# Attention with a warm-up on the identity, later gates, one transpose of the factors and another tie rule, and two blocks written out behind an expert's first

## The chip, the cores and the metric

One core of a Trainium2 chip runs one launch of the kernel. The metric is the time of one execution on the device in microseconds. Three executions of the kernel before took 898.0, 899.84 and 900.85 us (median 899.84).

## The reference, cut to what matters

Three steps follow one another, all in float32 on random inputs.

```python
# attention: q, k, v are (4, 8, 576, 64); M_prev, z_prev are a memory of each head
a = softmax(causal(q @ k.T / 8));  local = a @ v           # sum of exp + 1e-9 in the divisor
q_p = where(q > 0, q, exp(q) - 1) + 1
mem_out = (q_p @ M_prev) / (q_p @ z_prev + 1e-6)
x = g * mem_out + (1 - g) * local                          # g = sigmoid(beta), one for each head
# dense layer: 2304 tokens x 512, width 2048
h = x @ w_in;  x = (h * tanh(softplus(h))) @ w_out
# experts: 8 of width 1024, each token goes to its best one, or is left as it is
active = x @ w_skip > 0;  e = argmax(x @ w_gate);  gate = softmax(x @ w_gate)[e]
out = x;  out[active] += gate * relu(x @ w1[e]) @ w2[e]
```

On the inputs of the reference 225, 124, 333, 54, 528, 206, 18 and 5 tokens go to experts 0 to 7.

## The kernel before, in words

**Attention** works on 16 pairs of heads, p = 0 to 15. A pair has the steps that `attention` adds to a planner (`Work`, from L840): loads on SP's queue (`ld`, `lq`, `lv`, L939), the scaling of q on POOL (`sq`, L1014), the memory's q_p and its row sums (`f1` to `f4`), four score steps on TensorE (`S0` for query tiles 0 and 1, `S2`, `S3`, `S4`; L1046 to L1054), the row maximum on VectorE (`pk`, L1060 and L1063), the exponential with its row sum on ScalarE (`ex`, L1074), the factors of each row (`s0`, `s1`, `s2`: 1/sum times 1-g or g), the memory's part beside the exponentials (`place`, L1100), TensorE transposes of the exponentials by query tile (`t0` to `t4`, `b0`; L1106) with their evictions (L1006 on VectorE, L1008 on ScalarE), and the products with v and M (`AV0`, `AV1`, L1134), which leave the pair's output, turned, in the PSUM tile `px`. Two PSUM slots serve the scores (`ps`) and two the transposes (`pt`).

The output is still to be scaled by the factors, which stand along partitions and are wanted along the free dimension. So `r` transposes them on TensorE, three times (even heads, odd heads, the last half tiles; L1112, L1113), `re` evicts them in two pieces to `rt_`, `rw` stores these with two transfers to DRAM (L1122, L1123), and `rs` reads them back, spread over 64 partitions for each head, with two transfers (L1127). `xe` copies `px` to SBUF (VectorE or ScalarE), `X` multiplies by the spread factors `R` on POOL (L1146), `xo` stores. The last pair goes the same way.

Between these steps runs the conversion of the first weight matrix of the dense layer (`cv`, 16 pieces; L792, L803, L813 to L837) and, near the end, the loading and splitting of the first two token blocks (`xs`).

**The planner's order.** Every step has an engine, a duration, a due time (`key`; pairs are 11.2 apart) and the steps that it needs. `Work.run` repeatedly takes the step with the lowest rank, and the plan's order is each engine's program order:

```python
rank = (round((start + turn) * 8), t[0], t[1])
```

`start` is the time from which engine, needs and slot are free, `turn` a switch cost of TensorE, `t[0]` the due time: steps within the same eighth of a microsecond go by due time. The first loads of pair 0 are not in the plan, so that its steps count as ready at time 0. The gates (`g0`, `g1`, L984 to L996) are due at 4 and 5.

Ahead of the plan, VectorE clears 512 columns of an exponential's buffer (L1264) and TensorE multiplies it by itself twice (`keep_warm`, L1262); both results are never read.

**The dense layer** (`moe`) follows: for each block of 256 tokens `gemm1` (L197 to L199), the activation on ScalarE (L209 to L222), `gemm2` (L249 to L251). The first 16 steps convert the second weight matrix on the way (`convert`: L805, L813 to L824, L834 on ScalarE, L837 on POOL).

**The experts.** Two blocks of 128 tokens of the fullest expert run at the end of the dense layer. Then a loop over the 8 experts computes a first block, always, with the next expert's weights being split in between. Behind it stand `NSTAT - 1` further blocks inside nested conditionals on the expert's number of blocks `nb[e]`, read at run time, and behind them, in one more conditional, a run-time loop for the rest:

```python
for j in range(1, NSTAT):
    stack.enter_context(tc.If(nb[e] > j))
    if j + 1 < NSTAT:
        nxt["g"] = gather(idx(e, j + 1), j % 2)     # and turn it during the block
    block(e, xg, xT, idx(e, j), gate(e, j), fill)
stack.enter_context(tc.If(nb[e] > NSTAT))
with tc.For_i(NSTAT, nb[e], 1) as j:
```

So each written-out block but the last gathers and turns the rows of the next one, whether that runs or not. With the token counts above (the fullest expert's first 256 taken out) the experts have 2, 1, 3, 1, 3, 2, 1 and 1 blocks: six blocks behind an expert's first, two of them third blocks, no fourth.

## Time and profile before

| | |
|---|---|
| three executions | 898.0, 899.84, 900.85 us |
| the profiled execution | 903.65 us, of which the span is 901.9 us |
| TensorE | 844.4 us busy (94%), 5412 matmul instructions |
| TensorE's weight loads | 687.3 us (76%) |
| ScalarE | 622.4 us (69%) |
| VectorE | 577.8 us (64%) |
| POOL | 278.4 us (31%) |
[...]

Shares of busy time are means over three different stages: attention to about 235 us, the dense layer to about 665 us, the experts to the end. A row of the timeline gives start, duration, engine, line, operation, output and inputs, the number of instructions merged, and in brackets how long the engine sat idle before it and what ended that. PEld is TensorE's weight load, PEq and PEldq its sequencer, SPq the queue of DMA issues.

### The profile page before, as it was taken

How to read it: one execution, taken by the hardware profiler on the slowest of the kernel's cores; microseconds unless marked ns; L12 is line 12 of the kernel's file. 1: busy time of each engine (PE TensorE's matmuls, PEld its weight loads, DVE VectorE, ACT ScalarE, POOL GpSimd, SP SyncE). 2: the span in 40 equal slices, each digit the busy share in tenths (PEclk: the TensorE clock that was granted, in tenths of full speed). 3: DMA queues.
4: the chain of work that ended last, by engine and by line, in shares of the span. 5: the costliest groups of instructions: out<-in, count | busy, mean ns of one | idle time of the engine just before them, and what ended most of it. 6: DMA issues, size and time to landing. Idle time of an engine off the chain costs nothing.

```text
span 901.9 us, 15116 instructions
## 1 busy us (share of the span) xinstructions
PE 844.4 (94%) x5412; PEld 687.3 (76%) x5412; DVE 577.8 (64%) x1171; ACT 622.4 (69%) x1136; POOL 278.4 (31%) x358
## 2 busy tenths in 40 slices
PE   5899999999889999999999999999988989989995
PEld 3566656666779998989898989888866867768774
DVE  6988878766488843356575757575558666373661
ACT  4687768876588887787878788787845555363551
POOL 5876776854223230110111111011103212211200
PEclk8999999999999999999999999999989999999998
DMA  6666657642333231010101010122336958284610
GB/s 211 192 197 206 200 168 230 214 143 87 123 94 110 94 129 49 24 47 24 48 24 48 25 48 24 48 94 95 95 125 211 349 197 288 67 288 151 198 62 4
DMA packets 53704, 113.44 MB, mean 126 GB/s; under 512 B 12148, under 2 KB 17396, under 8 KB 53600
## 3 DMA queue, kind: packets, MB, share of 16 engines
q1 hardware_dynamic: 43968, 91.22, 31.3%
q0 software_dynamic: 4064, 10.42, 3.5%
q10 hardware_dynamic: 5568, 10.49, 3.2%
q8 instruction: 56, 0.92, 0.4%
q14 instruction: 48, 0.39, 0.1%
HBM read 94.47 MB, written 18.77 MB: 126 GB/s over the span
## 4 chain that ended last, share of the span: by engine, by line
PE 40%; DMA 21%; issue 15%; ACT 8%; POOL 7%; DVE 5%; SPq 1%; ACTq 0%; POOLq 0%; another core or an unknown queue 0%; DVEq 0%
DMA cvt<-yd,ids 8%; DMA out<-cvf,ids 6%; PE ph L197 6%; PE ph L199 6%; PE ph L198 6%; PE py L249 6%; PE py L251 6%; PE py L250 6%; DMA r<-rd 3%; DMA qn<-qn 2%; PE px L1134 2%; PE pt L1106 2%; POOL mn L1027 1%; ACT e L1074 1%; DVE nm L1063 1%
## 5 line engine op out<-in xcount | busy, mean ns | idle before, releaser
L197 PE MATMUL ph<-xh,u 128*128 128x256 f32 x576 | 163.8, 284 | 0.9 <-DVE xr L1006 0.9
L199 PE MATMUL ph<-xh,u 128*128 128x256 f32 x576 | 162.5, 282 | 0.0
L198 PE MATMUL ph<-xl,u 128*128 128x256 f32 x576 | 162.3, 282 | 0.0
L249 PE MATMUL py<-u,gh 128*128 128x512 f32 x288 | 115.8, 402 | 4.9 <-POOL u L837 4.9
L251 PE MATMUL py<-u,gl 128*128 128x512 f32 x288 | 115.7, 402 | 4.2 <-DVE gl L235 4.2
L250 PE MATMUL py<-u,gh 128*128 128x512 f32 x288 | 115.1, 400 | 0.0
L197 PEld LDWEIGHTS ph<-xh,u 128*128 128x128 f32 x576 | 109.8, 191 | 3.4 <-DVE xr L1006 1.1
L198 PEld LDWEIGHTS ph<-xl,u 128*128 128x128 f32 x576 | 109.8, 191 | 2.5
L199 PEld LDWEIGHTS ph<-xh,u 128*128 128x128 f32 x576 | 109.8, 191 | 0.0
L225 DVE SCALAR_TENSOR_TENSOR g<-t,g 128x512 f32<-128x512 f32 x72 | 49.9, 693 | 92.0 <-ACT t L221 89.8
L1074 ACT ACTIVATE e<-ps,nm 128x256 f32<-128x256 f32 (+4 forms) x144 | 78.0, 550 | 29.7 <-DVE nm L1063 21.9
L235 DVE TENSOR_TENSOR gl<-g,gh 128x512 fp32r<-128x512 f32 x72 | 51.1, 709 | 62.4 <-ACT gh L234 53.9
L1106 PE MATMUL pt<-ident,e 128*128 128x128 f32 x528 | 77.0, 285 | 8.3 <-ACT eta L1008 5.6
L351 POOL DMA_INDIRECT rt<-pay,sl x18 | 22.1, 1225 | 181.6 <-DVE pay L349 178.8
L209 ACT ACTIVATE g<-ph 128x512 f32<-128x512 f32 x72 | 42.7, 593 | 46.8 <-PE ph L199 45.8
L1106 PEld LDWEIGHTS pt<-ident,e 128*128 128x128 f32 x528 | 57.5, 143 | 18.6 <-ACT eta L1008 7.5
L251 PEld LDWEIGHTS py<-u,gl 128*128 128x128 f32 x288 | 54.9, 191 | 19.5 <-DVE gl L235 6.3
L249 PEld LDWEIGHTS py<-u,gh 128*128 128x128 f32 x288 | 55.2, 192 | 15.6 <-POOL u L837 5.0
L106 POOL TENSOR_TENSOR xl<-xr,xh 128x256 fp32r<-128x256 f32 x36 | 31.5, 880 | 112.0 <-ACT xh L105 111.8
L837 POOL TENSOR_TENSOR u<-cvf,u 128x512 fp32r<-128x512 f32 x32 | 46.6, 1458 | 58.6 <-ACT u L834 58.6
L250 PEld LDWEIGHTS py<-u,gh 128*128 128x128 f32 x288 | 54.9, 191 | 9.9
L1063 DVE TENSOR_REDUCE nm<-ps 128x2 f32<-128x256 f32 (+1 forms) x64 | 51.1, 816 | 7.0 <-PE ps L1054 6.1
(236 smaller groups left out, 1976.7 us busy)
## 6 DMA issues: line engine op xcount, KB each, us to landing
raw<-w SPq DMA_DIRECT2D x26, 512.0 KB
qk<-qk SPq DMA_DIRECT2D x16, 608.0 KB
raw<-w_in SPq DMA_DIRECT2D x16, 512.0 KB
raw<-w_out SPq DMA_DIRECT2D x16, 512.0 KB
xl<-w SPq DMA_DIRECT2D x16, 512.0 KB
xh<-w SPq DMA_DIRECT2D x15, 512.0 KB
qn<-qn SPq DMA_DIRECT2D x16, 384.0 KB
vx<-vx SPq DMA_DIRECT2D x16, 320.0 KB
```

What stands on the lines that cost most here:

```text
L197: T.matmul(ps[:, f2], win(HI, k, f), hi[:, k], start=(k == 0), stop=False)
L198: T.matmul(ps[:, f2], win(HI, k, f), lo[:, k], start=False, stop=False)
L199: T.matmul(ps[:, f2], win(LO, k, f), hi[:, k], start=False, stop=(k == KD - 1))
L225: V.scalar_tensor_tensor(out=g, in0=t, scalar=ROOT_HALF, in1=g, op0=ALU.add, op1=ALU.mult)
L235: V.tensor_tensor(out=gl, in0=g, in1=gh.bitcast(F32), op=ALU.subtract)
L249: T.matmul(ys[i][t], gh[:, f2, ts], wout(HI, f), start=(f == 0), stop=False)
L250: T.matmul(ys[i][t], gh[:, f2, ts], wout(LO, f), start=False, stop=False)
L251: T.matmul(ys[i][t], gl[:, f2, ts], wout(HI, f), start=False, stop=(f == KF - 1))
L837: self.nc.gpsimd.tensor_tensor(out=lo, in0=self.now.pop(i), in1=hi.bitcast(F32), op=ALU.subtract)
L1063: V.tensor_reduce(out=nm, in_=ps[:, :, o:o + w], axis=AX.X, op=ALU.max, negate=True)
L1074: A.activation(out=E[p % 2][:, k, 64:64 + w], in_=src, func=AF.Exp, bias=nm[:, h:h + 1], scale=1.0, accum_out=SS[p % 2][:, 0, k:k + 1])
L1106: T.transpose(ps[:, c], E[p % 2][:, k, j * 128:(j + 1) * 128], ident)
```

## The change

1. `NSTAT` goes from 5 to 3: two blocks are written out behind an expert's first instead of four, and the run-time loop starts at the fourth block.
2. The planner's rank becomes `start + turn + 0.05 * key`.
3. The factors are transposed at once into `[9, 128]`, evicted in one piece, stored with one transfer, and spread with four (for each head one with three pieces of 128 values in a row, and one of 64 values). The steps `r`, `re` and `rw` are due 1.2 to 1.3 us earlier, and their planned durations differ.
4. For the last pair, `xe` is on VectorE and multiplies `px` by `R` while evicting; the POOL step `X` is left out there.
5. The warm-up becomes 12 matmuls of the identity with itself, ahead of the first loads; the clearing of the 512 columns goes.
6. Pair 0's loads stand in the plan with their latencies, so its steps are planned behind them; the load of v moves to the front of the planned loads; `g0` needs `f1`, and `g1` is due at 7 and needs the row maximum of tile 2.

```diff
-NSTAT = 5
+NSTAT = 3
...
-                        rank = (round((start + turn) * 8), t[0], t[1])
+                        rank = (start + turn + 0.05 * t[0], t[0], t[1])
...
-        rd = [dr.tile([2, S], F32, name=f"rd{i}") for i in range(2)]
+        rd = [dr.tile([NS, 128], F32, name=f"rd{i}") for i in range(2)]
...
-        rt_ = c1.tile([NQT, 3, 128], F32, name="rt")
+        rt_ = c1.tile([NS, 128], F32, name="rt")
...
+        for i in range(12):
+            T.matmul(px[:, 0, 0:128], ident, ident, start=True, stop=True)
         load(0, "qk")
         load(0, "qn")
...
-            r = rrs.pop(p)[:, 0]
+            T.transpose(ps[0:NS, 0], rrs[p][:, 0], ident)
+
+        def keep_r(e, p):
+            evac(e, rt_, pts.pop((p, "r"))[0:NS, 0])
+
+        def store_r(p):
+            SP.dma_start(out=rd[p % 2], in_=rt_)
+
+        def spread_r(p):
+            d = rd[p % 2]
             for h in range(2):
-                T.transpose(ps[0:NQT, h], r[:, h:2 * NQT:2], ident)
-            T.transpose(ps[0:1, 2], r[:, 2 * NQT:NS], ident)
...
+                SP.dma_start(out=R[p % 2][HS[h], 0:QW].rearrange("p (t q) -> p t q", t=NQT),
+                             in_=d[0:2 * NQT].rearrange("(t h) (a q) -> h a t q", h=2, a=1)[h].to_broadcast([64, NQT, 128]))
+                SP.dma_start(out=R[p % 2][HS[h], QW:S], in_=d[2 * NQT:NS, HS[h]].to_broadcast([64, 64]))
...
-            evac(e, xt, pxf[:, 256:256 + S])
+            if p < NPAIR - 1:
+                evac(e, xt, pxf[:, 256:256 + S])
+            else:
+                V.tensor_tensor(out=xt, in0=pxf[:, 256:256 + S], in1=R[p % 2], op=ALU.mult)
...
-        wk.add(("lv0",), "S", 0.5, 0.5, lambda: load(0, "vx"), lag=3.5)
-        wk.add(("g0",), "A", 0.25, 4.0, gates0)
-        wk.add(("g1",), "V", 2.1, 5.0, gates1, [("g0",)])
+        wk.add((0, "lq"), "S", 0.5, -30.0, lambda: load(0, "vx"), lag=4.5)
+        wk.add((0, "ld"), "G", 0.1, -30.0, lambda: None, lag=4.0)
+        wk.add(("g0",), "A", 0.25, 4.0, gates0, [(0, "f1")])
+        wk.add(("g1",), "V", 3.0, 7.0, gates1, [("g0",), (0, "pk", 2)])
...
-            wk.add(key("r"), "T", 0.35, o + P + 3.3, lambda p=p: turn_r(p), [key("s2", 0), key("s2", 1)], take="t")
-            wk.add(key("re"), "VA", 0.6, o + P + 3.7, lambda e, p=p: keep_r(e, p), [key("r"), prev("rw")], give="t")
-            wk.add(key("rw"), "S", 1.0, o + P + 4.0, lambda p=p: store_r(p), [key("re"), prev2("rs")], lag=3.3)
-            wk.add(key("rs"), "S", 1.0, o + P + 7.0, lambda p=p: spread_r(p), [key("rw"), prev2("X")], lag=3.0)
+            wk.add(key("r"), "T", 0.15, o + P + 2.0, lambda p=p: turn_r(p), [key("s2", 0), key("s2", 1)], take="t")
+            wk.add(key("re"), "VA", 0.25, o + P + 2.4, lambda e, p=p: keep_r(e, p), [key("r"), prev("rw")], give="t")
+            wk.add(key("rw"), "S", 0.5, o + P + 2.8, lambda p=p: store_r(p), [key("re"), prev2("rs")], lag=3.3)
+            wk.add(key("rs"), "S", 2.0, o + P + 7.0, lambda p=p: spread_r(p), [key("rw"), prev2("X")], lag=3.0)
...
+            end = p == NPAIR - 1
+            wk.add(key("xe"), "V" if end else "VA", {"V": 0.7, "A": 0.6}, o + P + 8.0, lambda e, p=p: out_x(e, p),
+                   [key("AV0"), key("AV1")] + [("xs", 1, KD - 1), key("rs")] * end + [prev2("xo")])
+            if not end:
+                wk.add(key("X"), "G", 1.5, o + P + 11.0, lambda p=p: scale_x(p), [key("xe"), key("rs")])
...
-        V.memset(wtile[:, 0:512], 0.0)
-        for _ in range(2):
-            keep_warm()
         wk.run()
```

## Rows read from the trace of the kernel before

**Rows 1.** Busy time of each engine by stretch: span, busy us, clock, DMA share.
```profile
20.00:60.00 40.00, 35.22 (x264) 23.10 (x264) 36.20 (x58) 28.76 (x83) 31.38 (x44) 0.93 0.64 196
60.00:120.00 60.00, 56.54 (x476) 37.38 (x474) 52.72 (x89) 45.77 (x135) 45.56 (x69) 0.98 0.63 197
```

**Rows 2.** Timeline of the start, all engines.
```profile
1.10 0.29 POOL masks.py:199 TENSOR_SCALAR_AFFINE_SELECT ident<-ident 128x128 f32<-128x128 f32 x1
...
5.08 0.88 POOL L1014 TENSOR_SCALAR qk<-qk,nums,one 128x640 f32<-128x640 f32 x1 [1.12 <-DMA qk<-qk]
...
5.79 3.53 PE L1262 MATMUL px<-e 128*128 128x512 f32 x4 [5.79 <-DVE e L1264]
...
7.97 0.17 DVE L987 TENSOR_SCALAR gates<-gates 128x12 f32<-128x12 f32 x1
...
9.24 0.49 PE L1051 MATMUL ps<-qk 64*128 64x128 f32 x4
...
11.62 0.16 DVE L996 COPY by<-gates 128x4 f32<-128x4 f32 x1
11.70 1.01 DVE L1063 TENSOR_REDUCE nm<-ps 128x2 f32<-128x256 f32 x2
...
15.86 1.23 DVE L1063 TENSOR_REDUCE nm<-ps 128x2 f32<-128x1024 f32 x1 [1.30 <-PE ps L1054]
```

**Rows 3.** Groups of instructions: count, busy us, mean ns, idle before.
```profile
L1112 PE MATMUL pt<-ident,rr 128*4 128x128 f32 x32 | 6.1, 272 | 4.5 <-DVE etb L1006 3.6 <-ACT etb L1008 0.7
...
L479 PE MATMUL py<-ident,y 128*128 128x128 f32 x24 | 3.6, 274 | 0.8 <-DMA y<-yd,ids 0.8
...
L1006 DVE COPY rt<-pt 4x256 f32<-4x256 f32 (+1 forms) x10 | 3.1, 340 | 0.7 <-PE pt L1113 0.5
```

**Rows 4.** Who waited for whom: total us, times, longest.
```profile
POOL xt L1146 <- DMA r<-rd: 23.6, 10, 5.2
```

**Rows 5.** Timeline from the last pair into the dense layer.
```profile
229.90 1.01 PE L1106 MATMUL pt<-ident,e 128*128 128x128 f32 x7 [0.35 <-DVE etb L1006]
...
231.49 0.38 PE L1112 MATMUL pt<-ident,rr 128*4 128x128 f32 x2 [0.59 <-DVE etb L1006]
...
231.91 2.49 PE L1134 MATMUL px<-etb,vx 128*64 128x320 f32 x20
...
232.78 0.60 SPq L1123 DMA_DIRECT2D rd<-rt  x1
...
234.43 1.11 SPq L1127 DMA_DIRECT2D r<-rd  x2
234.44 0.76 DVE L1006 COPY xr<-px 128x576 f32<-128x576 f32 x1 [1.81 <-PE px L1134]
...
235.26 0.39 PE L197 MATMUL ph<-xh,u 128*128 128x256 f32 x1 [0.86 <-DVE xr L1006]
...
235.83 0.28 PE L198 MATMUL ph<-xl,u 128*128 128x256 f32 x1
...
237.98 1.43 POOL L1146 TENSOR_TENSOR xr<-xr,r 128x576 f32<-128x576 f32 x1 [7.94 <-DMA r<-rd]
...
240.55 0.58 ACT L209 ACTIVATE g<-ph 128x512 f32<-128x512 f32 x1
...
251.87 0.77 PE L249 MATMUL py<-u,gh 128*128 128x512 f32 x1 [4.86 <-POOL u L837]
```

**Rows 6.** Branches of TensorE's sequencer: duration ns min/median/max.
```profile
L766 PEldq COMPARE_BRANCH  x18: 70/197/6063, 712.6 to 887.7; - x18
```

**Rows 7.** Timeline of TensorE among the experts.
```profile
743.99 0.47 PE L495 MATMUL ph<-u,ah 128*128 128x512 f32 x1 [2.12 <-PEq L766]
...
783.26 0.50 PE L495 MATMUL ph<-u,ah 128*128 128x512 f32 x1 [0.44 <-PEq L766]
...
799.32 0.47 PE L495 MATMUL ph<-u,ah 128*128 128x512 f32 x1 [2.88 <-PEq L766]
...
801.19 0.63 PE L496 MATMUL ph<-u,ah 128*128 128x512 f32 x1
```

More of the change, by code (lines that the diff above doesn't have):

```diff
@@ L1109, in turn_r @@
             pts[p, "r"] = ps = ps_t.tile([128, 4, 128], F32, name="pt")
-            r = rrs.pop(p)[:, 0]
-            for h in range(2):
-                T.transpose(ps[0:NQT, h], r[:, h:2 * NQT:2], ident)
-            T.transpose(ps[0:1, 2], r[:, 2 * NQT:NS], ident)
-        def keep_r(e, p):
-            ps = pts.pop((p, "r"))
-            evac(e, rt_[:, 0:2], ps[0:NQT, 0:2])
-            evac(e, rt_[0:1, 2], ps[0:1, 2])
-        def store_r(p):
-            d = rd[p % 2]
-            SP.dma_start(out=d[:, 0:QW].rearrange("h (t q) -> t h q", t=NQT), in_=rt_[:, 0:2])
-            SP.dma_start(out=d[:, QW:S].unsqueeze(0), in_=rt_[0:1, 2].rearrange("a (h q) -> a h q", h=2))
-        def spread_r(p):
-            for h in range(2):
-                SP.dma_start(out=R[p % 2][HS[h]], in_=rd[p % 2][h:h + 1].to_broadcast([64, S]))
+            T.transpose(ps[0:NS, 0], rrs[p][:, 0], ident)
[5 more added lines that the diff above has]
+            d = rd[p % 2]
+            for h in range(2):
+                SP.dma_start(out=R[p % 2][HS[h], 0:QW].rearrange("p (t q) -> p t q", t=NQT),
+                             in_=d[0:2 * NQT].rearrange("(t h) (a q) -> h a t q", h=2, a=1)[h].to_broadcast([64, NQT, 128]))
+                SP.dma_start(out=R[p % 2][HS[h], QW:S], in_=d[2 * NQT:NS, HS[h]].to_broadcast([64, 64]))
         def av(p, i):
@@ L1226, in attention @@
                    ev("t20", "t21", "t30", "t31", "t4", "b0") + [key("t4", "e", 1), key("b0", "e", 1)] + [prev("xe"), key("lv")])
-            wk.add(key("xe"), "VA", {"V": 0.7, "A": 0.6}, o + P + 8.0, lambda e, p=p: out_x(e, p),
-                   [key("AV0"), key("AV1")] + [("xs", 1, KD - 1)] * (p == NPAIR - 1) + [prev2("xo")])
-            wk.add(key("X"), "G", 1.7, o + P + 11.0, lambda p=p: scale_x(p), [key("xe"), key("rs")])
-            wk.add(key("xo"), "S", 0.5, o + P + 13.0, lambda p=p: store_x(p), [key("X")], lag=2.5)
+            end = p == NPAIR - 1
[3 more added lines that the diff above has]
+                wk.add(key("X"), "G", 1.5, o + P + 11.0, lambda p=p: scale_x(p), [key("xe"), key("rs")])
+            wk.add(key("xo"), "S", 0.5, o + P + 13.0, lambda p=p: store_x(p), [key("X"), key("xe")], lag=2.5)
         NCV = 16
@@ L1257, in attention @@
                 wk.add(("xs", x, k), "G", 1.2, t + 7.0 + 1.5 * k, lambda x=x, k=k: xs.split(x, k), [("xl", x)] + [("xs", x, k - 1)] * (k > 0))
-        wtile = E[1].rearrange("p a b -> p (a b)")
-        def keep_warm():
-            T.matmul(px[:, 0], wtile[:, 0:128], wtile[:, 0:512], start=True, stop=True)
-        V.memset(wtile[:, 0:512], 0.0)
-        for _ in range(2):
-            keep_warm()
         wk.run()
```

## The prediction

> **What bounds the kernel now.** I read the busy time by stretch first, because the whole span mixes three stages. In the middle of attention TensorE is busy 56.54 of 60 us, VectorE 52.72, ScalarE and POOL some 46 [rows 1]: TensorE sets the pace and VectorE is close behind. From 20 to 60 us TensorE has only 35.22 of 40 us and a clock of 0.93 [rows 1], so the start is not yet at that pace. The dense layer runs on TensorE without a gap and the change leaves it alone. So the change can count at four places: the start, the factors' work of each pair, the passage into the dense layer, and the ends of the experts' blocks. There I read the timeline.
>
> At the start the scaled q is ready at 5.96 us (5.08 + 0.88), yet the first score matmul starts at 9.24, when the warm-up that began at 5.79 has run out [rows 2]. VectorE then takes the first maximum only at 11.70, since the gates hold it from 7.97 to 11.78 (the merged rows overlap a little) [rows 2].
>
> At the passage the dense layer's first matmul waits for VectorE's copy of `px`, 0.86 us [rows 5]. POOL waits 7.94 us for the spread factors and multiplies at 237.98; the activation starts at 240.55, and TensorE then stands 4.86 us ahead of 251.87, because the conversion of the second weights is late [rows 5]. That conversion follows ScalarE, which writes where attention's tiles lay and starts once their last user, POOL at 237.98, is done.
>
> **The start, -2.5 us.** Four old warm-up matmuls of 512 columns take 3.53 us [rows 2], 1.72 ns a column. The new ones are 12 calls of two instructions (as the two old calls gave four) of 128 columns: 3072 columns, 5.3 us at that rate. They need only the identity, ready at 1.39 us [rows 2], and end at 6.7. Scores then start at 6.7 instead of 9.24: 2.5 us. The gates' 3.8 us are moved and not removed: what was queued behind them on VectorE, the maxima, comes first; behind them now stand the maximum of tile 3 and the factors of pair 0. That bounds the gain below: until the maximum of tile 3 at 15.86 VectorE has the same work and loses only its 1.30 us of idling [rows 2]. Above, the first maximum could come 3.9 us sooner (6.7 plus 1.1 of scores is 7.8, against 11.70). I take 2.5, the advance of the scores. The cleared 512 columns cost VectorE something that nobody waits for any more. Planning pair 0 behind its loads puts v ahead of pair 1's q on SP's queue; its 0.5 us of issue lies beside the other loads, and if q came late by that, POOL would lose it once.
>
> **The factors, -3.5 us.** Three small transposes go from 231.49 to the next TensorE instruction at 231.91 [rows 5], 0.14 us each; two fewer in 16 pairs are 32 x 0.14 = 4.5 us. The step also waits 4.5 us in all for evictions to free a slot [rows 3]: a saved matmul ahead of such a wait is worth nothing, but a slot held for one eviction less may shorten the wait itself. So the ends are 0 and 9. TensorE is busy 94% of the time, which is nearest to the 4.5; I take 3.5. The 16 evictions that fall away are 0.34 us each on VectorE [rows 3], 5.4 us over two engines; I cost them at nothing of their own, since TensorE covers them. The spread now has four issues on SP: two cost 1.11 us [rows 5], so the last piece leaves 1.1 us later; the second store (0.60) [rows 5] goes, and the step is due 1.3 us earlier. On balance `R` comes 0.8 us sooner, and SP's loads wait 0.5 us more. POOL waits 23.6 us for `R` at ten pairs [rows 4], with `sum`, `place` and the next q's scaling queued behind it; POOL has 14 us in 60 to spare [rows 1], so I count nothing. No row shows transfers in pieces of 512 bytes; bounds are no cost, or once more the 2.4 us from the last issue's end (235.54) to POOL's start at 237.98 [rows 5], at each pair. The same POOL idling covers all but that excess; I take none, and leave 2 us of it to the range.
>
> **The tie rule, 0.** Two steps a pair apart differ by 11.2 in due time, thus 0.56 us of start; before, one eighth. The plan will now let an engine stand up to half a microsecond for an older pair's step. Which orders this gives cannot be read from the trace. From above the gain is the idle time that is left, some 3.5 us in each 60 [rows 1]; I allow 4 us either way.
>
> **The passage, +1.5 us.** The step `r` of the last pair is now due ahead of the last seven transposes, which start at 229.90. So take the factors there instead of at 231.49 [rows 5], one eviction and one store of the same latency (the store went at 232.78, and the spread followed at 234.43, 1.65 us later [rows 5]): the spread starts at 232.35, its four issues end at 234.55, and 2.4 us later, at 237.0, VectorE multiplies for 0.76 us [rows 5]. `px` is free at 237.7, and the dense layer's first matmul moves from 235.26 to 237.7 [rows 5]. Five of its matmuls take 0.57 us (235.26 to 235.83), so the 24 of the first step 2.7: they end at 240.4, just before ScalarE takes them up today, at 240.55 [rows 5]. POOL's 1.43 us are gone from the front of the conversion, but ScalarE gains nothing by that while it waits for TensorE. Add that TensorE has by then stood 3.3 us: after 2.88 us of standing, the matmul of 799.32 takes 0.47 us and that of 801.19 0.63 [rows 7], at the low clock. Some ten at that price are 1.6 us more. The ends are 0 and 2.5, the whole delay; I take 1.5. Unmoved, `r` comes 1.6 us later, with the clock's part on top 4.
>
> **The experts, -2.1 us.** Two third blocks run, and each gathers and turns a fourth block that never does. Of 24 such transposes (six blocks of four) 8 go, 3.6 / 24 = 0.15 us each [rows 3]: 1.2 us. Their evictions and two gathers lie beside the matmuls. TensorE's sequencer runs ahead of its matmuls, but a skip costs it up to 6063 ns where the median branch takes 197 [rows 6], and TensorE stands: 2.12 and 2.88 us where four blocks are skipped, 0.44 where two are, and much the same at the other experts with a second block (four in all) [rows 7]. The distance falls from four, three or two skipped blocks to two, one or none. Nothing in the trace shows so short a skip; the bounds are no gain, and all of it, 2.12 + 2.88 + 4 x 0.44 = 6.8 us. Skipping two blocks stalled, so single-block experts, which now skip as many, keep theirs; of the four others I take half, 0.9 us.
>
> [...]
>
> **Sum.** -2.5 - 3.5 + 1.5 - 2.1 = -6.6 us. The profiled execution took 903.65 us, 901.9 of it span and 1.75 around it, and lies 3.8 us above the median of the three. Its sum is 897.05; against the median of 899.84 it is **893.2 us**. Differences under 0.3%, 2.7 us, cannot be told from none here, so faster is below 897.1 and slower above 902.5.
>
> **The rivals.**
> - *All skips become short.* For it: the skipped code is about halved. Against: a skip of two blocks already stalled. It adds 5.9 us: 887.3. Chance 0.12.
> - *The start is swallowed.* Pair 2's loads wait for pair 0's buffers and the pipeline refills at VectorE's pace; TensorE's low clock up to 60 us speaks for it, the 1.30 us of idling against. Then the start gives 1.3 and the factors 1.5: -1.3 - 1.5 + 1.5 - 2.1 = -3.4 and, with 1 us lost to the smaller pieces, 897.4. Chance 0.16.
> - *The plan does not move `r`.* The moved due time stays without effect where the step waits for a slot, as it does for 0.59 us at 231.49 [rows 5]. The passage then costs 4: 895.7. Chance 0.10.
> - *The new rank makes TensorE stand* (slower). Once a pair it stands for an older step; the price is up to 0.56 us each time, and a step that arrives later than planned doubles it. It decides from (6.6 + 2.7) / 16 = 0.58 us a pair on. At 0.75 a pair, 12 us: 905.2. For it: the planner's costs are shorter than the measured ones. Against: half of the stand would have been a wait for a slot anyhow. Chance 0.11.
>
> **How the numbers follow.** The forecast itself has 0.51. Faster takes it, the short skips and the unmoved `r`: 0.73. Same is the swallowed start, 0.16. Slower is the rank, 0.11. The range runs from 886, the short skips with a little from the tie rule, to 900, the swallowed start and the upper ends of the passage and of the smaller pieces; it leaves out the slower case and some tails.
>
> **What would show it.** In the profile after, the first score matmul stands near 6.7 us and the first maximum near 8; there is one matmul with `rr` in each pair and one eviction to `rt`; the dense layer's first matmul waits 3 us or more for VectorE's multiplication, and the wait of 4.86 is shorter; the transposes from the gathered rows are 16 instead of 24, and the gaps behind the experts' skips are as they were or half as long. I am wrong if attention's end relative to its start of scores does not come 3 us sooner, if the gaps behind single-block experts vanish, or if TensorE's idling from 60 to 180 us grows by more than 4 us.

## The result and the profile after

The kernel after takes 888.89 us (median of 4 runs, 886.51 to 890.08) against 900.02 us for the kernel before in the same comparison: ratio 0.985, 95% interval 0.9814 to 0.9886, so 11.1 us less. 893.2 us were predicted, with a range of 886 to 900; the sign and the range hold, but two terms of the sum were far off and another came to nothing, so that the time lies in the range partly by luck (see below). The profiled execution took 887.86 us (span 886.1 us). Between the two profiles the difference is 15.8 us, more than between the medians, since the profile of before lies 3.6 us above its median and this one 1.0 below its own. What follows splits the 15.8.

| mark in the profile | before | after | difference |
|---|---|---|---|
| first score matmul | 9.24 | 6.55 | -2.7 |
| last product of the first pair (`AV1`) begins | 33.38 | 30.24 | -3.1 |
| that of the second pair | 49.62 | 42.69 | -6.9 |
| that of the third pair | 64.23 | 56.28 | -8.0 |
| that of the last pair | 231.91 | 223.35 | -8.6 |
| dense layer's first `gemm2` (L249) | 251.87 | 245.06 | -6.8 |
| experts' first wait for `h0l` ends | 695.78 | 686.53 | -9.3 |
| end of the span | 901.9 | 886.1 | -15.8 |

So attention gave 8.6 us, nearly all of it within its first three pairs; the passage took 1.8 back; the dense layer gave 2.4 and the experts 6.5. From the third pair to the last the lead grows by 0.6 us only. The change leaves the dense layer's code alone, and over all the kernels run its stretch from L249 to `h0l` takes 441.4 to 443.9 us (443.9 here before, 441.5 after): the 2.4 us are not shown to be of the change.

Busy time by stretch, the columns as in [rows 1]; the first row is that of the kernel before, for a stretch that [rows 1] does not have, the others are of the kernel after:

```profile
8.00:20.00 12.00, 7.47 (x54) 4.31 (x53) 10.39 (x27) 5.55 (x18) 6.96 (x9) 0.82 0.49 192
...
8.00:20.00 12.00, 5.42 (x36) 3.11 (x32) 7.46 (x25) 5.55 (x18) 5.34 (x9) 0.72 0.49 191
20.00:60.00 40.00, 38.53 (x311) 25.31 (x311) 39.10 (x63) 29.86 (x86) 29.96 (x46) 1.00 0.65 205
60.00:120.00 60.00, 56.72 (x474) 37.61 (x472) 56.64 (x91) 44.67 (x129) 48.77 (x69) 1.00 0.67 205
```

Between 20 and 60 us TensorE is busy 38.53 us where it was 35.22, and its clock is 1.00 instead of 0.93 [rows 1]. From 60 to 120 us it is as busy as before (56.72 against 56.54) at a clock of 1.00 instead of 0.98; VectorE and POOL do more there.

The timeline of the start, as in [rows 2]:

```profile
1.45 5.18 PE L943 MATMUL px<-ident 128*128 128x128 f32 x24 [1.45 <-POOL ident masks.py:199]
6.55 0.49 PE L1053 MATMUL ps<-qk 64*128 64x128 f32 x4
...
7.85 1.88 DVE L1065 TENSOR_REDUCE nm<-ps 128x2 f32<-128x256 f32 x3
...
11.88 0.69 ACT L1019 ACTIVATE mn<-qn 128x576 f32<-128x576 f32 x1 [4.63 <-DMA qn<-qn]
...
13.18 0.35 ACT L1076 ACTIVATE e<-ps,nm 128x128 f32<-128x128 f32 x1
...
14.94 2.08 PE L1053 MATMUL ps<-qk 64*128 64x512 f32 x4 [6.37 <-ACT e L1076]
```

Scores and maxima come as early as predicted. Yet the first exponential is at 13.18, where before it was at 12.80: ahead of it in ScalarE's order stands a step of pair 1 (L1019, `f1`), which waits 4.63 us for that pair's q. So TensorE stands 6.37 us ahead of the fourth query tile, and the clock of 8 to 20 us falls from 0.82 to 0.72.

The groups that answer to [rows 3], and the wait of [rows 4]:

```profile
L1112 PE MATMUL pt<-ident,rr 128*9 128x128 f32 x16 | 4.4, 273 | 1.6 <-DVE etb L1008 0.8 <-POOL cvt L803 0.7
...
L1010 ACT ACTIVATE rt<-pt 9x128 f32<-9x128 f32 x12 | 3.1, 259 | 2.0 <-PE pt L1112 2.0
...
L479 PE MATMUL py<-ident,y 128*128 128x128 f32 x16 | 2.4, 275 | 0.7 <-DMA y<-yd,ids 0.7
```

```profile
POOL xt L1147 <- DMA r<-rd: 3.8, 5, 1.1
```

One transpose of the factors a pair is left, their evictions went mostly to ScalarE, and POOL waits 3.8 us for the spread factors instead of 23.6: the four smaller pieces cost nothing that shows.

The passage, as in [rows 5]:

```profile
223.35 2.49 PE L1132 MATMUL px<-etb,vx 128*64 128x320 f32 x20 [0.78 <-DVE etb L1008]
...
227.77 0.76 DVE L1142 TENSOR_TENSOR xr<-px,r 128x576 f32<-128x576 f32 x1 [4.48 <-DMA r<-rd]
...
228.58 0.58 PE L197 MATMUL ph<-xh,u 128*128 128x256 f32 x1 [2.75 <-DVE xr L1142]
...
233.00 0.60 ACT L209 ACTIVATE g<-ph 128x512 f32<-128x512 f32 x1 [3.10 <-PE ph L199]
...
245.06 0.74 PE L249 MATMUL py<-u,gh 128*128 128x512 f32 x1 [3.46 <-POOL u L837]
```

TensorE waits 2.75 us for VectorE's multiplication, its first matmul takes 0.58 us (0.39 before) at a granted clock of 0.50 from 228.5 to 231.4 us (1.00 before, 235.2 to 236.0), and ScalarE now waits 3.10 us for TensorE where it came without a wait before.

The experts: branches and semaphore waits of TensorE's sequencer (ns). First the kernel before from 770 to 785 us, then the kernel after in two stretches, 727 us and 760 to 774 us, and the matmuls behind them, as in [rows 6, 7]:

```profile
L766 PEldq COMPARE_BRANCH  x2: 193/1741/3289, 779.2 to 783.0; - x2
...
L766 PEldq EVENT_SEMAPHORE  x1: 51/51/51, 782.9 to 782.9; - x1
```

```profile
L766 PEldq COMPARE_BRANCH  x1: 6049/6049/6049, 727.4 to 727.4; - x1
...
L766 PEldq COMPARE_BRANCH  x2: 193/266/339, 769.2 to 772.5; - x2
...
L766 PEldq EVENT_SEMAPHORE  x1: 51/51/51, 772.4 to 772.4; - x1
```

```profile
733.59 0.77 PE L495 MATMUL ph<-u,ah 128*128 128x512 f32 x1 [2.88 <-PEq L766]
...
772.80 0.50 PE L495 MATMUL ph<-u,ah 128*128 128x512 f32 x1 [0.44 <-PEq L766]
...
787.72 0.47 PE L495 MATMUL ph<-u,ah 128*128 128x512 f32 x1 [1.75 <-PEq L766]
```

Experts 1 and 3, with one block, still pay 2.88 and 1.75 us (expert 6, also with one, pays 0.38). At 772 us, where only the run-time loop is skipped now, the branch takes 339 ns and not 3289 as in the kernel before, and yet the gap is the same 0.44 us. The rows show why: before, the skip ran from 779.2 to 782.5 us, beside the block's last matmuls, which end at 782.82. Only then come the semaphore wait at 782.9 and a second branch of 193 ns at 783.0, and the next matmul at 783.26; the kernel after has the same two ahead of 772.80. So the gap of 0.44 us was never the skip's.

### The profile page after: what moved, and what is told of

Same layout as the page of the kernel before. It is cut to its first block, busy times and chain, and to the rows that moved or that the text cites. A ratio compares the mean times of both kernels' runs of the same rounds, so it can differ in the third digit from the quotient of the medians.

```text
span 886.1 us, 15038 instructions
## 1 busy us (share of the span) xinstructions
PE 839.3 (95%) x5392; PEld 685.0 (77%) x5392; DVE 577.7 (65%) x1164; ACT 617.9 (70%) x1122; POOL 276.3 (31%) x355
## 5 line engine op out<-in xcount | busy, mean ns | idle before, releaser
L249 PE MATMUL py<-u,gh 128*128 128x512 f32 x288 | 115.8, 402 | 3.5 <-POOL u L837 3.5
L1076 ACT ACTIVATE e<-ps,nm 128x128 f32<-128x128 f32 (+2 forms) x144 | 78.1, 552 | 20.8 <-DVE nm L1065 12.0
L251 PEld LDWEIGHTS py<-u,gl 128*128 128x128 f32 x288 | 54.9, 191 | 18.6 <-DVE gl L235 5.3
L249 PEld LDWEIGHTS py<-u,gh 128*128 128x128 f32 x288 | 55.2, 192 | 14.1 <-POOL u L837 3.6
L1053 PE MATMUL ps<-qk 64*128 64x128 f32 (+3 forms) x256 | 51.8, 490 | 6.8 <-ACT e L1076 6.8
```

The source lines that it names most:

```text
L249: T.matmul(ys[i][t], gh[:, f2, ts], wout(HI, f), start=(f == 0), stop=False)
L251: T.matmul(ys[i][t], gl[:, f2, ts], wout(HI, f), start=False, stop=(f == KF - 1))
L1053: T.matmul(ps[:, h, o:o + w], ts[HS[h], t * 128:(t + 1) * 128], ts[HS[h], KO:KO + w], start=True, stop=False)
L1076: A.activation(out=E[p % 2][:, k, 64:64 + w], in_=src, func=AF.Exp, bias=nm[:, h:h + 1], scale=1.0, accum_out=SS[p % 2][:, 0, k:k + 1])
```

## The experiments

u_tie, u_plan, u_fac and u_nstat ran on one chip, t_noturn, b_tie, u_last and n_shift on a second, and u_warm, b_nstat, early and best on a third, each beside the kernel before, to which the ratio is taken. u_tie, u_plan, u_fac, u_nstat, u_last and u_warm each undo one of the six parts in the kernel after. Numbers are in us; `AV1`, L249 and span are of one profiled execution each.

| run | edit | median | ratio to before, 95% | last `AV1` | L249 | span |
|---|---|---|---|---|---|---|
| after | | 888.89 | 0.985 [0.9814, 0.9886] | 223.35 | 245.06 | 886.1 |
| u_tie | old tie rule | 901.01 | 1.0014 [0.999, 1.0037] | 231.67 | 253.74 | 900.0 |
| u_plan | part 6 undone | 890.54 | 0.9894 [0.9859, 0.9928] | 224.41 | 246.33 | 889.3 |
| u_fac | part 3 undone | 895.22 | 0.9928 [0.9896, 0.9959] | 225.20 | 250.00 | 894.7 |
| u_nstat | NSTAT 5 | 907.95 | 1.007 [1.0025, 1.0114] | 224.16 | 247.45 | 907.7 |
| t_noturn | old rule, no switch cost | 898.21 | 0.9969 [0.9941, 0.9996] | 229.80 | 250.24 | 892.2 |
| b_tie | before, new rule alone | 897.98 | 0.9986 [0.9955, 1.0016] | 221.64 | 241.62 | 895.4 |
| u_last | part 4 undone | 888.05 | 0.9842 [0.9775, 0.9909] | 223.17 | 241.76 | 885.7 |
| n_shift | NSTAT 5, code moved | 894.95 | 0.9929 [0.9904, 0.9955] | 222.73 | 244.69 | 893.3 |
| u_warm | part 5 undone | 883.91 | 0.9757 [0.9713, 0.9802] | 223.22 | 243.70 | 884.1 |
| b_nstat | before, NSTAT 3 alone | 896.91 | 0.9926 [0.9894, 0.9958] | 230.85 | 250.76 | 893.8 |
| early | `px` copied first | 886.35 | 0.9817 [0.977, 0.9864] | 222.11 | 240.69 | 884.1 |
| best | early, other start | 881.85 | 0.9762 [0.9718, 0.9807] | 218.41 | 237.00 | 878.1 |

Three of them have the attention of the kernel after (after, u_nstat, n_shift), and their last `AV1` spreads over 1.4 us; before and b_nstat share theirs too, 1.1 us apart. Differences of that size at this mark say nothing. Nor do small ones at the experts: from `h0l` to the end of the span the ten kernels with NSTAT 3 take 198.6 to 204.7 us, with the same blocks written out.

**The tie rule: u_tie, t_noturn, b_tie.**

```diff
u_tie:    -rank = (start + turn + 0.05 * t[0], t[0], t[1])
          +rank = (round((start + turn) * 8), t[0], t[1])
t_noturn: +rank = (round(start * 8), t[0], t[1])
b_tie (kernel before):
          -rank = (round((start + turn) * 8), t[0], t[1])
          +rank = (start + turn + 0.05 * t[0], t[0], t[1])
```

> The changed kernel with the old rank (eighths of a microsecond, then due time). The prediction counted the tie rule at nothing, within 4 us: 885 to 893, likeliest 889. Theory 'rank': the rank is what makes the order of the first pairs better, so undoing it gives 894 to 897 with TensorE's idling from 20 to 60 us back near 4 us (1.5 in the changed kernel, 4.8 before).

Undoing this one line takes back everything: 901.01 us, no different from before. Not all of it is the order's, as far as is shown: of the 13.9 us between the two profiles 5.1 lie at the experts (204.7 us from `h0l` on against 199.6), where the blocks are the same, TensorE's clock is 0.96 instead of 0.98 and its waits are 1.7 us longer; why stays open. The last `AV1` falls back by 8.3 us, and 6.4 of them are lost by the second pair (49.11 against 42.69). TensorE's timeline shows how, first of u_tie, then of the kernel after; L1048 is the score step `S4`, L1053 `S2` and `S3`, L1132 the products:

```profile
23.27 1.20 PE L1048 MATMUL ps<-qk 128*128 128x512 f32 x4
...
26.36 0.92 PE L1053 MATMUL ps<-qk 64*128 64x384 f32 x4
...
28.96 1.26 PE L1048 MATMUL ps<-qk 128*128 128x512 f32 x4 [0.94 <-POOL qk L1016]
...
31.78 1.13 PE L1053 MATMUL ps<-qk 64*128 64x512 f32 x4
...
32.95 2.49 PE L1132 MATMUL px<-etb,vx 128*64 128x320 f32 x20
```

```profile
23.66 0.92 PE L1053 MATMUL ps<-qk 64*128 64x384 f32 x4
...
27.53 1.13 PE L1053 MATMUL ps<-qk 64*128 64x512 f32 x4
...
29.09 1.19 PE L1048 MATMUL ps<-qk 128*128 128x512 f32 x4
...
30.24 2.49 PE L1132 MATMUL px<-etb,vx 128*64 128x320 f32 x20
```

By the old rule `S4` of the next pair goes ahead of that pair's `S2` and `S3`, and at 28.96 one of a pair further on, for which TensorE even waits 0.94 us, stands ahead of the first pair's `AV1`. It takes one of two score slots and time on ScalarE from the older pair. By the new rule the order is one pair after the other. Waits of TensorE, 20 to 235 us, in u_tie (us in total, times, longest):

```profile
PE pt L1108 <- ACT etb L1010: 4.4, 8, 0.9
PE ps L1048 <- ACT e L1076: 3.4, 4, 1.2
PE pt L1108 <- DVE etb L1008: 3.3, 4, 1.4
PE pt L1108 <- ACT eta L1010: 2.8, 4, 1.2
```

These rows and the smaller ones sum to 20.4 us. In the kernel after, without the wait at the passage, the same view sums to 10.1; its longest rows are

```profile
PE pt L1108 <- DVE eta L1008: 2.8, 7, 0.8
...
PE px L1132 <- DVE etb L1008: 2.7, 3, 1.1
```

The 10.3 us between them cover the 8.3 at the last `AV1`.

> The changed kernel with the old rank, but without the switch cost in it: the start in eighths, then the due time. With the old rank whole the changed kernel took 901.0 us, 12 more, and TensorE's order there has the score step S4 of the next pair (same array mode as the transposes, so no switch cost) ahead of that pair's S2 and S3 and of the older pair's products. Theory 'switch': it is the switch cost of 0.1, which moves a start into another eighth and so beats any difference in due time, that lets S4 overtake; without it the attention ends within 2 us of the changed kernel's: last AV1 at 223 to 226, total 888 to 892. Theory 'weight': what is needed is the due time's weight over longer waits; then last AV1 stays near 231 and the total near 900.

Without the switch cost the old rule stays bad: the last `AV1` is at 229.80, only 1.9 us better than in u_tie, and that in an execution at the low end of this kernel's runs (893.91, median 898.21). So it is not the switch cost that brings the late steps forward; what is left of the old rule is that a due time counts for nothing unless two starts fall within an eighth of a microsecond.

> The kernel before with the new rank alone. Theory 'rank alone': the attention ends 7 to 9 us sooner, last AV1 at 223 to 225, total 5 to 8 us under the kernel before. Theory 'together': the rank needs the true latencies of pair 0 and the shorter factors' step; then it gives 0 to 4 us. The experts' stage is that of the kernel before in either case, unless TensorE's code, which is moved by some instructions, lies otherwise to the fetched blocks.

Alone in the kernel before, the new rule brings the last `AV1` to 221.64, 10.3 us sooner, and `gemm2` 10.3 us sooner too. From 20 to 60 us:

```profile
20.00:60.00 40.00, 38.27 (x307) 25.14 (x306) 35.73 (x59) 30.48 (x88) 29.79 (x45) 0.99 0.57 187
```

That is the 38.53 us and the clock of the kernel after, without its other parts. With the old rule, then, the other parts leave the last `AV1` where it was (231.67 in u_tie, 231.91 before), and with the new one it comes 1.7 us sooner without them than with them (221.64 against 223.35): attention's gain is the rule's. But the time falls by no more than can be told from nothing (4.0 us by the medians, with an interval that includes no change): the experts, from `h0l` on, take 211.6 us (683.79 to 895.4) where before took 206.1, with two waits that end in "issue" (2.23 us at 853.80, 2.03 at 871.58) that before does not have. The section on NSTAT comes back to these.

**The start: u_warm, u_plan, best.**

```diff
u_warm:  -12 matmuls of ident with itself, ahead of the first loads
         +V.memset(wtile[:, 0:512], 0.0) and two matmuls of wtile, as in the kernel before
u_plan:  -(0, "lq"), (0, "ld") in the plan; g0 needs f1; g1 due at 7, needs (0, "pk", 2)
         +("lv0",) due at 0.5; g0 due at 4 and g1 at 5, as in the kernel before
best:    +pair 1: its loads 2.0 and 2.5 earlier, lag 7.5 for 4.5 and 3.5
         +pair 0: load of v due at 2.0 in place of -30.0 (and the edit of early)
```

> The kernel after with the old warm-up (512 columns cleared by VectorE, two products of them) in place of the 12 on the identity. Theory 'queue': ScalarE's first exponential stands behind the step f1 of pair 1, which waits for that pair's loads until about 13 us, so when the scores start makes nearly no difference: the first score matmul goes back to about 9.3 us, the first AV1 stays within 1 us of 30.24, and the time is 0 to 1.5 us above the kernel after. Rival 'start' (the prediction's term): all 2.5 us come back, AV1 of the first pairs stands 2.5 us later and the time is 891 to 892.

The scores go back to 9.36, and nothing follows from it: the first `AV1` is at 29.79 (30.24 in the kernel after), the last at 223.22. The 12 matmuls on the identity bring nothing here. The kernel is not slower but, at 0.9757, faster than the kernel after in its own comparison; that ratio comes from another chip, and beside early and best on the same chip its runs (879.85 to 885.86) lie with those of best. Half of the 2.0 us between the two profiles lies at the experts, where its waits behind branches are 1.8 us in all instead of 6.8. Whether the old warm-up is itself a little better stays open; that the new one gains 2.5 us in this kernel is out.

> The changed kernel with part 6 undone: pair 0's loads are not in the plan, v's load and the gates are where they were. The profile of the changed kernel has the first score matmul at 6.55 us but the third tile's maximum at 17.27, later than before (15.86), and yet the first AV1 is 3.1 us and the third 8.0 us earlier than before. Theory 'start' (the prediction's): the start's gain is the scores' advance, half of which the gates' move brings; undone, the kernel loses 1 to 2.5 us: 890 to 891.5. Theory 'plan': the gain in the filling of the pipeline (7 to 8 us by the third pair) comes from planning pair 0 behind its loads: 895 to 897, and the third AV1 near 64 us instead of 56. Theory 'factors': no more than 1 us.

1.1 us at the last `AV1`, within the spread of equal programs, and 0.9894 against 0.985 in intervals that overlap. Planning pair 0's loads and moving the gates is worth about a microsecond at most. Its profile shows what part 6 trades: here ScalarE's first exponential, at 12.67, waits 5.42 us for VectorE's maximum, which stands behind the gates, and pair 1's step comes after it, at 14.27. Part 6 takes the gates out of the way, but in its order pair 1's step stands ahead of the exponential and holds it until 13.18, though that pair's q is issued at the same time (3.65 us, here 3.69).

> As 'early', and pair 1's loads are issued ahead of v of pair 0 and planned with a longer latency, so that f1 of pair 1 does not stand ahead of pair 0's exponentials on ScalarE. Theory 'queue': ScalarE's first exponential starts near 9.5 us instead of 13.2, the score step S3 near 11.5 instead of 14.9, the first AV1 near 28; of that 1 to 3 us are left at the last AV1 and the time is 883 to 886. Rival 'pace': VectorE's maxima set the start, the first AV1 is within 1 us of 30.24, and the time equals that of 'early'.

Here pair 1's step does not stand in the way; ScalarE and TensorE at the start:

```profile
9.00 0.37 ACT L1076 ACTIVATE e<-ps,nm 128x128 f32<-128x128 f32 x1 [1.72 <-DVE nm L1065]
...
11.71 0.70 ACT L1019 ACTIVATE mn<-qn 128x576 f32<-128x576 f32 x1
```

```profile
10.77 1.31 PE L1053 MATMUL ps<-qk 64*128 64x512 f32 x4 [2.80 <-DVE gates L990]
```

The first exponential starts 4.2 us sooner than in the kernel after, the fourth query tile likewise (10.77 against 14.94), the first `AV1` at 26.73, and of these 3.5 us all are still there at the end: the last `AV1` is 3.7 us sooner than in early, which has the same passage. So the start can be worth what was predicted for it; what swallowed it was one step of another pair in ScalarE's order. How much of the 3.5 us needs the early scores is not shown, as best was not run with the old warm-up. With 881.85 us (879.82 to 885.28) best is by its median the fastest version run; early ran at 886.35 (885.89 to 891.18) beside it.

**The factors: u_fac.** Part 3 undone: three transposes, two evictions, two stores and two spreading transfers for each pair, with their old due times.

```diff
-T.transpose(ps[0:NS, 0], rrs[p][:, 0], ident)
+for h in range(2):
+    T.transpose(ps[0:NQT, h], r[:, h:2 * NQT:2], ident)
+T.transpose(ps[0:1, 2], r[:, 2 * NQT:NS], ident)
...
-wk.add(key("r"), "T", 0.15, o + P + 2.0, ...)
+wk.add(key("r"), "T", 0.35, o + P + 3.3, ...)
```

> The changed kernel with part 3 undone: three transposes, two evictions, two stores and two spreads of the factors for each pair, at the old due times. The prediction's term: 3.5 us more, 892.4, by TensorE's time alone. Theory 'factors': the earlier landing of R is what counts, because POOL waited 23.6 us for R in the kernel before and 3.8 in the changed one, and SP's loads stood behind the store that waits for POOL's multiplication: 895 to 899 with POOL's waits for R back at 15 us or more. Theory 'plan': 0 to 2 us.

The last `AV1` comes 1.9 us later, the dense layer's `gemm2` 4.9 us later. So of this part about 2 us lie in the pairs, just outside the spread, and 3 us at the passage, where VectorE's multiplication waits for `R`: its way from the last `AV1` to `gemm2` is 24.8 us against 21.7. That way varies, though: in the seven kernels that have both part 3 and part 4 it takes 20.4 to 23.3 us.

**The passage: u_last, early.**

```diff
u_last: -else: V.tensor_tensor(out=xt, in0=pxf[:, 256:256 + S], in1=R[p % 2], op=ALU.mult)
        +the copy of px by xe and the POOL step X for the last pair too
early:  +the copy of px at once for the last pair too, then
        +V.tensor_tensor(out=xts[p], in0=xts[p], in1=R[p % 2], op=ALU.mult)
```

> The changed kernel with part 4 undone: the last pair's output is copied from PSUM at once and multiplied by the factors on POOL. Theory of the prediction: the passage costs 1.5 us in the changed kernel, so this is faster by up to 1.5: TensorE's first matmul of the dense layer waits 0.9 us instead of 2.75, ScalarE's first activation there waits for no matmul, but POOL's 1.43 us come back ahead of the conversion. Rival: the multiplication on VectorE is worth its place, since the conversion starts 0.7 us sooner: this is slower by 0.5 to 1.

From the last `AV1` to `gemm2` it takes 18.6 us, where the kernel after takes 21.7 and before took 20.0 [rows 5]. Part 4 costs 3.1 us; the earlier factors give 1.4 back, which is the difference that the table at the top shows as 1.8. The two parts depend on each other: with neither the way is 20.0 us, with the factors alone 18.6, with part 4 alone (u_fac) 24.8, with both 21.7. Beyond `gemm2` most of it is lost again in this execution (the span is 0.4 us shorter than that of the kernel after), and its interval says nothing against equality.

> The kernel after, but the last pair's px is copied as soon as its products are done, and VectorE multiplies the copy by R afterwards. Theory 'passage': the dense layer's first matmul comes 2 us sooner after the last AV1 than in the kernel after (gap 0.9 in place of 2.75), while VectorE's multiplication still spares POOL's; gemm2 starts 2 to 3 us sooner, near 242, and the time is 885 to 887. Rival 'R': the activation and the conversion wait for the multiplication anyhow, gemm2 starts within 1 us of 245.06, and the time is that of the kernel after.

The passage of early, on all engines:

```profile
224.64 0.76 DVE L1008 COPY xr<-px 128x576 f32<-128x576 f32 x1 [2.59 <-PE px L1132]
...
225.45 0.39 PE L197 MATMUL ph<-xh,u 128*128 128x256 f32 x1 [0.86 <-DVE xr L1008]
...
226.43 0.76 DVE L1144 TENSOR_TENSOR xr<-xr,r 128x576 f32<-128x576 f32 x1 [1.03 <-DMA r<-rd]
```

`px` is free as soon as it is copied, TensorE waits 0.86 us and starts with a matmul of 0.39 us, as in the kernel before [rows 5], and the multiplication follows beside it: again 18.6 us from the last `AV1` to `gemm2`. What freed `px` mattered, not which engine multiplies. The time, 886.35, cannot be told from that of the kernel after: the 4.4 us that `gemm2` is ahead end as 2.0 us of span, as TensorE waits at the experts for other things (1.98 us for `kbh` at 701.98, 1.62 us for gathered rows at 714.07).

**NSTAT: u_nstat, n_shift, b_nstat.**

```diff
u_nstat: -NSTAT = 3
         +NSTAT = 5
n_shift: +NSTAT = 5, and ahead of the experts' counts being read
         +for _ in range(32): T.matmul(pr[:, 0], tri, cum, start=True, stop=True)
b_nstat (kernel before):
         -NSTAT = 5
         +NSTAT = 3
```

> The changed kernel with four blocks written out again. The prediction's term: 2.1 us more (1.2 for the two unused turnings, 0.9 for branches). The changed kernel's profile has TensorE's gaps behind the experts' conditionals nearly as before (0.44 at experts 2 and 4, although the sequencer's branch there fell from over 3 us to 0.34), so the branches should give nothing visible: 0.7 to 1.5 us more, 889.6 to 890.4. If shorter branches matter at single-block experts: 2 to 4 us more.

Far more than the 2.1 us: 907.95, and from `h0l` on 217.8 us (689.91 to 907.7) where the kernel after takes 199.6 and before 206.1, with the same experts' code as before. TensorE's matmuls there, and the branch ahead of the first:

```profile
742.00 0.79 PE L495 MATMUL ph<-u,ah 128*128 128x512 f32 x1 [6.91 <-issue]
...
803.95 0.79 PE L496 MATMUL ph<-u,ah 128*128 128x512 f32 x1 [3.83 <-issue]
```

```profile
L766 PEldq COMPARE_BRANCH  x1: 6229/6229/6229, 731.7 to 731.7; - x1
```

The branch ends at 738.0 and yet the matmul comes at 742.00; the wait of 3.83 us stands between two matmuls of a run that need nothing new. "issue" means that the engine waited for nothing that the profile shows. Behind both waits the matmuls take 0.63 us instead of 0.40; 0.63 is what the matmul of 801.19 takes in the kernel before [rows 7], at a granted clock of 0.50 (801 to 804 us).

> The changed kernel with four blocks written out (907.95 us, 19 more than the changed one) and 32 matmuls of 8 columns ahead of the experts' loop, 64 instructions of TensorE, which move all its later code by 4 KB and cost 3 to 4 us themselves. Theory 'place': in the run with four blocks TensorE stood 6.91 and 3.83 us without any release shown behind the skips of single-block experts, because the place that it skips to lies shortly ahead of the end of a fetched piece of code and the next piece had to be fetched too; moved by 4 KB, those waits fall to the 2 to 3 us of the other kernels, and the experts' stage is 4 to 9 us shorter in spite of the added work. Theory 'length': four blocks cost as much wherever the code lies; the two waits stay and the total is 910 to 912.

32 small matmuls more, whose only use is that TensorE's later code lies elsewhere, make the kernel 13 us faster: 0.9929 against 1.007; of the 14.4 us between the two profiles 11.0 lie from `h0l` on. No wait ends in "issue" any more, TensorE's time from `h0l` to its last matmul falls from 207.2 to 196.2 us, and the place of the earlier 6.91 reads

```profile
735.64 0.47 PE L495 MATMUL ph<-u,ah 128*128 128x512 f32 x1 [2.44 <-PEq L770]
```

So in this pair of runs the code's place decides, by 13.0 us of the medians where the whole change gains 11.1. The traces show the code coming: among the DMA transfers are some of the kind `instruction`, those on queue 8 all of 16 KB (56 in the kernel before, 52 in the one after), and in the dense layer, over 20 of them, one comes for every 256.4 instructions of TensorE in the kernel before and for every 256.5 in the one after. By estimate from these numbers that is 64 bytes an instruction, and 4 KB for the 64 instructions of the 32 matmuls. In u_nstat, from 738 to 742 us, when the branch is over and TensorE still stands (queue, kind, packets, MB, share):

```profile
q8 instruction: 1, 0.02, 1.7%
```

It runs from 739.57 to 740.67 us, and the matmul follows 1.33 us after its end; the one before it, 735.31 to 736.59, lies within the branch. So it is at each of the experts' waits of a microsecond or more that ends in "issue": 801.54 to 802.62 ahead of the matmul at 803.95, the two of b_tie, and one of 1.04 us in u_warm; the matmul comes 1.3 to 1.5 us after the transfer's end. In n_shift the second transfer at that branch runs from 739.36 to 740.30 us, while the matmuls from 735.64 on go on without a wait.

In the dense layer such transfers come with no such wait: from 262 to 655 us the kernels before and after have 19 of them each, and TensorE has no wait there that ends in "issue". The kernel after has them at that branch as well: 730.93 to 732.03 within its 6049 ns, and 735.84 to 736.96 while the matmuls from 733.59 go on without a wait. In u_nstat TensorE stands (6.91 and 3.83 us) until the transfer behind the branch is over. That the code at the branch's target goes over from one fetched piece to the next just there is the author's guess from these times; no row shows it.

> The kernel before with NSTAT = 3 alone. Attention stays as before (last AV1 near 231.9). Theory 'parts': the tail behind the last matmul falls from 10.7 to 8.5 us, eight transposes go (1.2 us) and the gaps lose some 1 us, so the time falls by 4 to 6 us, to 894 to 896. Theory 'prediction': 2.1 us less, 898. Theory 'place': a code position that is bad by chance gives gaps that end with issue at the experts, 4 to 7 us each, and takes back all of it.

6.2 us less by the medians, 8.1 between the spans, 1.1 of these in attention's spread. From `h0l` on 199.95 us against 206.1 before: 2.3 at the end, behind the last matmul (8.4 us to the end of the span against 10.7), and 3.9 in TensorE's stretch. Of the 3.9, TensorE's busy time makes 1.95 (187.63 before, 185.68 now), 1.2 of it by the eight transposes, and shorter waits the rest (the rows overlap a little): gathered rows 0.8, `h0l` 0.3, and 1.3 behind the branches, whose waits were 7.1 us in all before:

```profile
PE ph L495 <- PEq L766: 5.8, 7, 2.2
...
795.14 0.48 PE L495 MATMUL ph<-u,ah 128*128 128x512 f32 x1 [1.50 <-PEq L766]
```

The 1.3 are all at this one gap, behind expert 3 with its single block, which was 2.88 us before; those of 0.44 stay at 0.43 or 0.44. The size of 6.2 us is not firm: from `h0l` on the four kernels with NSTAT 5 take 206.1 to 217.8 us, and those with 3 take 198.6 to 204.7. The sign is.

## Why the prediction was right and where it was wrong

**The tie rule, 0 within 4 us either way.** This step failed. It measured 8.3 us at the last `AV1` in u_tie and 10.3 in b_tie, alone more than the whole predicted sum. The bound was taken from the idle time that is left in the steady state, as if the order could only fill gaps there. The rule does save some of that: between 60 and 180 us TensorE idles 11.0 us in u_tie against 5.9 in the kernel after, and 6.7 in the kernel before against 3.3 in b_tie, so 3 to 5 us, about the size allowed. But 6.6 of the 8.3 us, and 7.3 of the 10.3, are there by the third pair. The gain lies mainly in the first 60 us, where the pipeline fills and late pairs' scores were let in ahead of an older pair's; the row for that stretch, with 35.22 of 40 us at a clock of 0.93 [rows 1], was read and put down to the start. The slower rival built on this rule did not happen.

**The experts, -2.1.** Right in sign and in the transposes (1.2), under-sized at 6.2. The branches' 0.9 was half of the gaps at four experts with a second block; that reading failed, since those gaps of 0.44 us are a semaphore wait and a second branch behind the last matmul, and stay. The branches did give 1.3 us in b_nstat, but at one expert with a single block, which was to keep its gap. The end behind the last matmul (2.3), the waits for data (1.1) and shorter matmuls (0.7) were no terms of the sum. It also took the code's place for given: u_nstat and n_shift differ by 13 us with the same blocks written out.

**The rival of short skips** was half right in the row and wrong in the time: the skip ahead of 772 us costs 339 ns in place of 3289, and nothing is gained, since the longer one was already hidden behind matmuls. Experts 1 and 3 kept gaps of 2.88 and 1.75 us in the kernel after, where they had 2.12 and 2.88.

**The start, -2.5.** Matmuls and maxima came where they were forecast (6.55 and 7.85, for 6.7 and 8), the gain did not: u_warm shows 0. The step looked at TensorE and VectorE and not at ScalarE's order, where pair 1's `f1` waits for a transfer; the late q of pair 1 was thought of, but as a loss of POOL's. The swallowed-start rival had the outcome with another cause: neither VectorE's pace nor the clock (0.93 from 20 to 60 us [rows 1]) sets it, since in best 3.5 us came through.

**The factors, -3.5.** The working counted matmuls saved, 4.5 us. In the pairs u_fac shows 1.9, and only beside the new rule, for in u_tie the last `AV1` is that of the kernel before. That `R` comes sooner at the passage, some 3 us, was put into the next term.

**The passage, +1.5.** Measured +1.8, with the mechanism as described: a wait for the multiplication, matmuls at a granted clock of 0.50, ScalarE waiting for TensorE, a shorter wait ahead of `gemm2` (3.46 for 4.86). Undone alone it is 3.1, so the term was the net of two. Part 4 without the earlier factors (u_fac) costs 4.8, near the 4 of the rival with `r` unmoved.

The sum of -6.6 was thus too small by the tie rule's 8 and the experts' 4, and too large by the start's 2.5 and by 1.6 in the factors of the pairs. None of the three signs of being wrong came: attention from the first score to the last `AV1` is 5.9 us shorter, the gaps behind single-block experts are there, and TensorE's idling from 60 to 180 us did not grow. That the time still lies in the range is partly luck: the range went down to 886 for the short skips, which gained nothing, and it was the tie rule, at twice its bound, that filled it. In the medians 11.1 us came of it. The terms are read from single executions; the stretches of the table add up to the 15.8 between two profiles, of which the dense layer's 2.4 belong to no term.

## What to carry to other kernels

In a plan written by rank, look at the fill of the pipeline first: if a due time decides only between equal starts, younger work takes the slots of older work, and the delay is carried to the end. An early start on one engine is worth only what the order of the next engine lets through, so read that order up to the first step that waits for a transfer. Where code branches at run time, measure a change of its length with the rest moved as well, for the place of the code alone can be worth more than the edit (here 13.0 us, against the 6.2 of NSTAT in b_nstat).

## What was not expected of the hardware

- TensorE standing with nothing in these rows to wait for: 6.91 and 3.83 us behind taken branches in u_nstat, 2.23 and 2.03 in b_tie, none in n_shift, with the same experts' blocks in all three. A 16 KB transfer of instructions ends 1.3 to 1.5 us before each of these waits does.
- The end of the span behind TensorE's last matmul: 10.6 to 10.7 us in the four kernels with NSTAT 5, 8.4 to 8.6 in the ten with 3. It goes with the number of written-out blocks; why was not tried.
- A gap of 0.44 us at the end of an expert's blocks, the same whether the skip takes 339 or 3289 ns: it is made by a semaphore wait (51 ns) and a further branch (193 ns) that start when the last matmul has ended.
